# The second feed-forward level by seven products of halves in place of eight

## The chip, the cores and the metric

The kernel runs on one core of one Trainium2 chip. The metric is the device time of one execution in microseconds, the median over runs. Before the change three runs took 691.23 us (median), 689.8 us and 694.35 us.

## What is computed

An attention block of a recurrent kind (4 batches, 8 heads, 768 time steps, head size 40) is followed by a feed-forward block. Its output, seen as a matrix of 3072 tokens by 320, is the input x of the second block:

```python
for t in range(S):
    y[:, :, t] = einsum('bhd,bhde->bhe', rt, state)
    Sa = einsum('bhde,bhe->bhd', state, at)
    state = state * wt - einsum('bhd,bhe->bhde', Sa, bt) + einsum('bhd,bhe->bhde', vt, kt)
x = y.transpose(0, 2, 1, 3).reshape(B * S, H * D)      # 3072 x 320
h = x @ w_in                                           # 320 x 2048, given in float64
g = h * (1 / (1 + exp(-h)))
return g @ w_out                                       # 2048 x 320, given in float64
```

The last line is the second feed-forward level: per 256 tokens a product of 256 x 2048 by 2048 x 320, in fp32.

## The kernel before

The 768 time steps are cut into `NN` = 12 chunks of `C` = 64 steps. One chunk has 4 batches x 64 = 256 tokens. A chunk goes through these functions:

- `load` and `load_r` fetch the inputs of a chunk from HBM with SP's queue (from L402). k and b land in the staging tile `kbv` (L412).
- `prepare` (from L456) forms running products of w with two scans on VectorE (L473 and L491), multiplies a, k and b by them (L500 and L510; L510 reads `kbv` and writes the packed tile `kb`), and lets TensorE form products of `kb` with a (L528), mask them (L577), multiply them with v (L592) and transpose k and b (L617). Its result `R` goes to one of three buffers.
- `special` and `inverse` solve the triangular systems of a chunk: `special` for the first three chunks one at a time, `inverse` for two chunks at a time, with 19 steps of VectorE each (L643 and L644).
- `merge`, `chain` and `read` (from L940) put the inverse together, carry the state from chunk to chunk (L1046 to L1174) and read the output y (L1204 to L1269). L1269 writes y, and `bring` moves it by way of HBM to the tile `xt`, channels on partitions.
- `moe` (from L1332) is the feed-forward block. Its first level, in four groups of 512 hidden units, is L1340 and L1353 on TensorE and the Silu on ScalarE (L1363), which writes the tile `gts`: 16 blocks of 128 hidden units by 256 tokens. Its second level (`second`, L1380) takes, for each half `b` of 128 tokens, 16 products of a 128 x 128 block of `gts` (the stationary operand) with a 128 x 320 block of `wo` (the moving operand), summed in PSUM; each half is copied out to the tile `ot` (L261 on VectorE, in the last chunk L257 on ScalarE) and stored (L1399).
- `weights` turns w_in and w_out from float64 words into fp32 on the chip, in ten units, during the first chunks (from L314). `wo` is the converted w_out.

All these functions do not issue instructions; they add operations to a `Plan`, each with the engine, the keys of what it reads and writes, and the PSUM rooms that it needs. The order in which they are issued is written out by hand: `ORDER` (L74) lists the numbers of the operations, and `SLOTS` gives each room its buffer. Every engine and each DMA queue takes its own operations in this order and waits, at each, for what it needs. So a wait on one engine holds up all that is listed behind it on that engine.

fp32 products show in the profile as two TensorE instructions each, and each of these has its own load of the stationary operand (the rows named PEld).

Of the kernel before, what the change touches and what calls it, by code (L numbers as in the profile page):

```python
# [10 lines left out]
F32 = mybir.dt.float32  # L11
# [119 lines left out]
"""  # L131

SLOTS = """
02010313103013023201121220321321331102201331232212021000300010012010102103230113332111021202013323111302020230
10211001211003132011132330130003220300213021120013103110133031021231131031100212001201232130132032033001101332
32011022330030001301001320110132012332222001102003101210203231232113030320232121101130100132012
"""


@with_exitstack  # L140
def kernel(
    ctx: ExitStack,
    tc: tile.TileContext,
    aT: bass.AP,
    kT: bass.AP,
    bT: bass.AP,
    wT: bass.AP,
    rT: bass.AP,
# [14 lines left out]
    T = B * C  # L163
# [292 lines left out]
    def prepare(n):  # L456
# [1152 lines left out]
```

## Time and profile before

| what | number |
|---|---|
| median of three runs | 691.23 us (689.8 to 694.35) |
| span of the profiled execution | 690.3 us |
| instructions | 27487 |
| ScalarE busy | 198.4 us (29%) |
| mean granted TensorE clock | 0.994 |
| bytes read from and written to HBM | 60.03 and 14.35 MB |
| mean busy share of the 16 DMA engines, SP's queue | 36.0% |

How to read the lines of the profile that follow: a group is a line of the kernel, an engine, an operation, the tile written and the tiles read, the shape and the count; behind the bar stand the busy time of the group in us, the mean duration of one in ns, and how long the engine was idle just before, with what ended that. For TensorE `128*128` is the size of the stationary operand (rows by columns) and `128x320` that of the moving one. Times on TensorE are latencies of single instructions that run overlapped; the busy time of a group counts overlapped time once. PE is the matmuls, PEld the weight loads. In the timeline a row is the start in us, the time covered, and the group, with neighbours of one kind merged (`x48`).

### The profile page before, as it was taken

How to read it: one execution, taken by the hardware profiler on the slowest of the kernel's cores; microseconds unless marked ns; L12 is line 12 of the kernel's file. 1: busy time of each engine (PE TensorE's matmuls, PEld its weight loads, DVE VectorE, ACT ScalarE, POOL GpSimd, SP SyncE). 2: the span in 40 equal slices, each digit the busy share in tenths (PEclk: the TensorE clock that was granted, in tenths of full speed). 3: DMA queues.
4: the chain of work that ended last, by engine and by line, in shares of the span. 5: the costliest groups of instructions: out<-in, count | busy, mean ns of one | idle time of the engine just before them, and what ended most of it. 6: DMA issues, size and time to landing. Idle time of an engine off the chain costs nothing.

```text
span 690.3 us, 27487 instructions
## 1 busy us (share of the span) xinstructions
PE 656.6 (95%) x12794; PEld 531.4 (77%) x12794; DVE 420.9 (61%) x632; ACT 198.4 (29%) x254; POOL 13.0 (2%) x30
## 2 busy tenths in 40 slices
PE   1589999999999999999999999999999999999996
PEld 1467788788778778878778778778788778788774
DVE  7998988984894558954538962639854773011000
ACT  4562364343214332214222222222223122121020
POOL 3000110000000000000000000000000000000000
PEclk9999999999999999999999999999999999999999
DMA  9945385725255462561730672352542214111100
GB/s 291 296 125 138 92 257 168 183 37 133 78 140 120 103 167 63 128 159 27 194 103 14 193 166 66 104 134 74 152 86 65 74 35 105 28 45 34 42 2 22
DMA packets 113282, 76.64 MB, mean 111 GB/s; under 512 B 61154, under 2 KB 109589, under 8 KB 112520
## 3 DMA queue, kind: packets, MB, share of 16 engines
q1 hardware_dynamic: 110436, 63.71, 36.0%
q0 software_dynamic: 2224, 10.63, 4.7%
q8 instruction: 102, 1.67, 1.0%
q10 hardware_dynamic: 500, 0.46, 0.3%
q14 instruction: 20, 0.16, 0.1%
HBM read 60.03 MB, written 14.35 MB: 108 GB/s over the span
## 4 chain that ended last, share of the span: by engine, by line
PE 87%; DVE 7%; DMA 2%; issue 1%; SPq 1%; ACT 1%; POOL 1%; DVEq 0%; ACTq 0%; POOLq 0%
PE pair L1380 31%; PE pair L1340 24%; PE pair L1353 7%; PE pair L1204 4%; PE pair L528 3%; PE pair L1258 3%; PE pair L1158 2%; PE pair L617 2%; PE pair L1046 2%; PE pair L592 2%; PE pair L1243 2%; PE pair L1070 1%; PE pair L1101 1%; PE pair L890 1%; DVE kbv L473 1%
## 5 line engine op out<-in xcount | busy, mean ns | idle before, releaser
L1380 PE MATMUL pair<-wo,gts 128*128 128x320 f32 x768 | 215.8, 437 | 0.0
L1380 PEld LDWEIGHTS pair<-wo,gts 128*128 128x128 f32 x768 | 143.4, 190 | 58.0 <-issue 1.0
L1340 PE MATMUL pair<-xt,wi 128*128 128x256 f32 x768 | 175.8, 383 | 0.0
L1340 PEld LDWEIGHTS pair<-xt,wi 128*128 128x128 f32 x768 | 143.5, 190 | 22.1 <-issue 0.7
L1363 ACT ACTIVATE gts<-pair 128x1024 f32<-128x1024 f32 x48 | 47.6, 1026 | 91.2 <-PE pair L1353 84.1
L644 DVE TENSOR_REDUCE XI<-XI 128x64 f32<-128x512 f32 (+9 forms) x85 | 58.7, 690 | 2.9
L1216 DVE TENSOR_TENSOR lam<-pair,ml 128x1024 f32<-128x1024 f32 x22 | 26.4, 1220 | 46.6 <-PE pair L1204 29.4
L1353 PE MATMUL pair<-xt,wi 64*128 64x256 f32 x384 | 48.0, 389 | 0.8 <-DMA xt<-X 0.8
L261 DVE COPY ot<-pair 128x320 f32<-128x320 f32 x22 | 10.8, 489 | 57.0 <-PE pair L1380 49.4
L528 PE MATMUL pair<-a,kb 40*64 40x64 f32 x1536 | 30.1, 228 | 15.0 <-DVE a L500 13.4
L1353 PEld LDWEIGHTS pair<-xt,wi 64*128 64x128 f32 x384 | 35.3, 187 | 7.1 <-issue 2.0
L528 PEld LDWEIGHTS pair<-a,kb 40*64 40x64 f32 x1536 | 26.9, 141 | 17.2 <-issue 15.0
L643 DVE TENSOR_TENSOR XI<-XI,mi 128x1024 f32<-128x1024 f32 (+8 forms) x60 | 33.6, 560 | 5.1 <-DMA mi<-md 3.8
L510 DVE TENSOR_TENSOR kb<-kbv 128x512 f32<-128x512 f32 (+1 forms) x36 | 29.9, 862 | 6.6 <-PE pair L528 3.3
L630 ACT COPY kt<-pair 128x640 f32<-128x640 f32 x24 | 16.5, 695 | 56.1 <-PE pair L617 55.9
L1204 PEld LDWEIGHTS pair<-r,vut 40*64 40x64 f32 x1536 | 24.4, 135 | 5.2 <-issue 2.8
L473 DVE TENSOR_TENSOR_SCAN kbv<-wz,zt 128x1024 f32<-128x1024 f32 x12 | 27.5, 2292 | 0.6
L1204 PE MATMUL pair<-r,vut 40*64 40x64 f32 x1536 | 26.8, 220 | 1.0 <-DMA r<-in_rT 0.9
L491 DVE TENSOR_TENSOR_SCAN wz<-wz,zt 128x1024 f32<-128x1024 f32 x12 | 27.5, 2289 | 0.3
L259 ACT ACTIVATE vut<-pair 128x1024 f32<-128x1024 f32 (+1 forms) x13 | 12.5, 958 | 49.4 <-PE pair L1101 45.4
L643 DVE TENSOR_TENSOR XI<-XI,xs 128x1024 f32<-128x1024 f32 (+1 forms) x25 | 25.2, 1008 | 0.6
L937 ACT COPY mi<-XI 128x1024 f32<-128x1024 f32 x5 | 10.0, 2002 | 51.8 <-DVE XI L644 31.7
(160 smaller groups left out, 685.2 us busy)
## 6 DMA issues: line engine op xcount, KB each, us to landing
wz<-in_wT SPq DMA_DIRECT2D x12, 512.0 KB
a<-in_aT SPq DMA_DIRECT2D x12, 512.0 KB
kbv<-in_bT SPq DMA_DIRECT2D x12, 512.0 KB
kbv<-in_kT SPq DMA_DIRECT2D x12, 512.0 KB
vut<-in_vT SPq DMA_DIRECT2D x48, 96.0 KB
r<-in_rT SPq DMA_DIRECT2D x48, 96.0 KB
vu<-in_v SPq DMA_DIRECT2D x24, 160.0 KB
xh<-lam SPq DMA_DIRECT2D x22, 160.0 KB
```

The lines of the kernel that those rows point to most:

```text
L473: nc.vector.tensor_tensor_scan(back(V), back(W[:, 2 : 2 + Q * C]), zt, 1.0, ALU.mult, ALU.add)
L491: nc.vector.tensor_tensor_scan(Z, Z, zt, 0.0, ALU.mult, ALU.add)
L510: TTn[engine].tensor_tensor(out=at_(kb, place(is_b, first), (576 * step, 4 // step), (128, 4), (1, C)), in0=blocks((kf, bf)[is_b]), in1=bl ...
L528: nc.tensor.matmul(room.tile[half(b), j, g * C : g * C + C], lhsT=kb[rows(j), place(is_b, q) : place(is_b, q) + C], rhs=A[rows(j), q * C : ...
L643: nc.vector.tensor_tensor(out=at_(tmp, 0, *dims), in0=x, in1=y, op=ALU.mult)
L644: nc.vector.tensor_reduce(out=out_, in_=at_(tmp, 0, *dims), axis=AX.X, op=ALU.add)
L1204: nc.tensor.matmul(pl.tile[half(1 - b if role else b), b, c * C : c * C + C], lhsT=vut[rows(b), role, hu, :], rhs=rs[rows(b), hh, :], star ...
L1216: lambda pl=pl, la=la: nc.vector.tensor_tensor(out=la.tile.rearrange("p (q t) -> p q t", q=Q), in0=pl.tile.rearrange("p a b -> p (a b)").r ...
L1340: nc.tensor.matmul(rooms[g].tile[:, f // 2, (f % 2) * T : (f % 2) * T + T], lhsT=wi[:, k, (4 * g + f) * 128 : (4 * g + f) * 128 + 128], rh ...
L1353: nc.tensor.matmul(rooms[g].tile[:, h, (f % 2) * T : (f % 2) * T + T], lhsT=wi3[half(h), g * 256 + (f % 2) * 128 : g * 256 + (f % 2) * 128 ...
L1363: nc.scalar.activation(out=gts[:, 4 * g * T : 4 * g * T + 4 * T], in_=rooms[g].tile.rearrange("p a b -> p (a b)"), func=AF.Silu)
L1380: nc.tensor.matmul(po[b].tile[:, 0, 0:DM], lhsT=g4[:, f, 128 * b : 128 * b + 128], rhs=wo[:, f, :], start=f == 0, stop=f == NF - 1,)
```

## The change

From chunk 1 on, the second level is done by Strassen's algorithm (in Winograd's form). The 256 x 2048 matrix of gated values is cut into four blocks, by half of the hidden units and half of the tokens, and w_out into four of 1024 x 160. Instead of eight products of such blocks there are seven. Each is eight matmuls of a 128 x 128 stationary block with a 128 x 160 moving block (`prod`, `block_`). VectorE forms four sums of blocks of `gts`, in place (`mixed` on `gs`), and puts the seven products together in `ot`, which now holds a whole chunk. Three sums of blocks of w_out are made once, after chunk 0, into the tiles `tw` and `raw0` (`parts_`), and a fourth in place in `wo`. Chunk 0 keeps the old second level.

Room for the new tiles comes from two others. `kbv` goes: k and b are loaded straight into `kb`, with four transfers each, and VectorE multiplies there in place; of `kbv` there stays the tile `ws` for the scan. `Rs` has two buffers instead of three. The output of a chunk is stored by two transfers of 160 KB instead of four of 80 KB. The keys of `gts` are split by token half. `ORDER` and `SLOTS` are new, with 1568 operations in place of 1437.

```diff
-    kbv = sb.tile([128, 3, Q * C], F32, name="kbv")
+    ws = sb.tile([128, Q * C], F32, name="ws")
+    tw = sb.tile([128, 12 * HM], F32, name="tw")
...
-    Rs = ring("R", 3, Q * D)
+    Rs = ring("R", 2, Q * D)
...
-    ot = ring("ot", 1, DM)
+    ot = sb.tile([128, 2 * DM], F32, name="ot")
...
+            if dst is None:
+                for m in range(B):
+                    dma(
+                        lambda m=m, src=src, is_b=name == "b": nc.sync.dma_start(
+                            at_(kb, place(is_b, 4 * m), (2 * C, 4), (1, C)), src[m, n].rearrange("p (q c) -> p q c", q=4)
+                        ),
...
-                TTn[engine].tensor_tensor(
-                    out=at_(kb, place(is_b, first), (576 * step, 4 // step), (128, 4), (1, C)),
-                    in0=blocks((kf, bf)[is_b]),
-                    in1=blocks(V),
-                    op=ALU.mult,
-                )
+                x = at_(kb, place(is_b, first), (576 * step, 4 // step), (128, 4), (1, C))
+                y = at_(V, first * C, (4 * C * step, 4 // step), (C, 4), (1, C))
+                TTn[engine].tensor_tensor(out=x, in0=x, in1=y, op=ALU.mult)
...
+        def block_(half_, b, right, bank, i, first):
+            for f in range(8):
                 nc.tensor.matmul(
-                    po[b].tile[:, 0, 0:DM],
-                    lhsT=g4[:, f, 128 * b : 128 * b + 128],
-                    rhs=wo[:, f, :],
-                    start=f == 0,
-                    stop=f == NF - 1,
+                    po.tile[:, bank, col(i)],
+                    lhsT=g4[:, 8 * half_ + f, 128 * b : 128 * b + 128],
+                    rhs=right(f),
+                    start=first and f == 0,
+                    stop=f == 7,
+                    skip_group_check=True,
                 )
...
+        mixed(gs(0, 1), lambda: gs(0, 0), gs(0, 1), ALU.subtract, gk(0, 0), gk(0, 1))
+        prod(1, 1, made(2), [("T", 2)], 0, 2, True)
+        prod(0, 0, own(0, 0), lo, 0, 0)
+        prod(1, 0, own(1, 0), hi, 0, 1)
+        mixed(gs(1, 1), lambda: gs(1, 1), gs(0, 1), ALU.subtract, gk(0, 1), gk(1, 1))
+        mixed(gs(0, 0), lambda: gs(1, 1), gs(0, 0), ALU.add, gk(1, 1), gk(0, 0))
+        mixed(gs(1, 0), lambda: gs(1, 0), gs(1, 1), ALU.subtract, gk(1, 1), gk(1, 0))
+        last = ot[:, col(3)]
+        add("ACT", act(HM), lambda: nc.scalar.copy(out=last, in_=po.tile[:, 0, col(0)]), [(po, 0)], [("ot", 3)], 10 * n, [po])
+        mixed(ot[:, col(0)], lambda: po.tile[:, 0, col(1)], last, ALU.add, [(po, 0), ("ot", 3)], [("ot", 0)], HM, [po])
+        prod(0, 1, made(0), [("T", 0)], 1, 1, True)
+        prod(1, 1, made(1), [("T", 1)], 1, 2)
+        prod(0, 0, own(0, 1), lo, 1, 0)
+        prod(1, 0, own(1, 1), hi, 0, 0, True)
+        mixed(last, lambda: po.tile[:, 1, col(2)], last, ALU.add, [(po, 1)], [("ot", 3)], HM, [po])
+        mid = ot[:, HM : 3 * HM].rearrange("p (x d) -> p x d", x=2)
+        mixed(
+            mid, lambda: po.tile[:, 1, 0 : 2 * HM].rearrange("p (x d) -> p x d", x=2), last.unsqueeze(1).to_broadcast([128, 2, HM]), ALU.add,
+            [(po, 1), ("ot", 3)], [("ot", 1), ("ot", 2)], 2 * HM, [po],
+        )
+        mixed(last, lambda: po.tile[:, 1, col(0)], ot[:, col(2)], ALU.add, [(po, 1), ("ot", 2)], [("ot", 3)], HM, [po])
+        mixed(
+            mid, lambda: at_(po.tile[:, 0, :], 0, (2 * HM, 2), (1, HM)), mid, ALU.add, [(po, 0)], [("ot", 1), ("ot", 2)], 2 * HM, [po]
+        )
+        store()
...
+        mixed(part_(0, 0, 8), own(1, 1), own(0, 1), ALU.subtract, [*lo, *hi], [("T", 0)])
+        for f in (0, 4):
+            mixed(part_(1, f, 4), part_(0, f, 4), own(0, 0, f, 4), ALU.add, [*lo, ("T", 0)], [("T", 1)] + ["raw0"] * (f > 0), 4)
+            mixed(part_(2, f, 4), own(1, 0, f, 4), part_(1, f, 4), ALU.subtract, [*hi, ("T", 1)], [("T", 2), "raw0"], 4)
+        mixed(own(0, 1), own(0, 1), own(0, 0), ALU.subtract, [], lo)
```

`prod` numbers below follow the order of these lines: products 1 to 3 read the halves as the gate left them, products 4 to 7 read at least one sum.

More of the change, by code (lines that the diff above doesn't have):

```diff
@@ L300 @@
         "B": [("wo", c) for c in (1, 2)],
-        **{f"G{i}": [("gts", 2 * i), ("gts", 2 * i + 1)] for i in range(2)},
+        **{f"G{i}": [("gts", g, b) for g in (2 * i, 2 * i + 1) for b in range(2)] for i in range(2)},
     }
@@ L458, in prepare @@
         i3, i2 = n % 3, n % 2
-        (kf, bf, V), (kk, bk, vk) = [kbv[:, i] for i in range(3)], ("k", "b", "V")
+        V, vk = ws, "V"
+        kk, bk = ([(x, m) for m in range(B)] for x in "kb")
         W, A = wz[i3], at[i3]
@@ L536, in prepare @@
         pb_ = Room("pair", 2)
-        add("PE", 0.9, partial(between, 1, pb_), ["B", ("a", i3)], [pb_, ("sb", i2)], pri, [pb_], 128)
+        add("PE", 0.9, partial(between, 1, pb_), [*bk, ("a", i3)], [pb_, ("sb", i2)], pri, [pb_], 128)
         add("ACT", act(1024), lambda: copy("ACT", sbs[i2], by_two(pb_.tile), -1.0), [pb_], [("sb", i2)], pri, [pb_])
@@ L573, in prepare @@
         pk, sk = Room("pair", 2), Room("lam", 3)
-        add("PE", 0.9, partial(between, 0, pk), ["K", ("a", i3)], [pk], pri + 0.5, [pk, sk], 128)
+        add("PE", 0.9, partial(between, 0, pk), [*kk, ("a", i3)], [pk], pri + 0.5, [pk, sk], 128)
         def masked():
@@ L598, in sv @@
                 )
-        add("PE", 0.9, sv, [sk, ("v", i2, 0), ("v", i2, 1)], [pv, ("R", i3)], pri + 0.6, [pv, sk], 128)
+        add("PE", 0.9, sv, [sk, ("v", i2, 0), ("v", i2, 1)], [pv, ("R", i2)], pri + 0.6, [pv, sk], 128)
         add(
@@ L603, in prepare @@
             act(640),
-            lambda: nc.scalar.copy(out=Rs[i3][:, 0 : Q * D].rearrange("p (b c) -> p b c", b=2), in_=pv.tile[:, :, 0 : 8 * D]),
+            lambda: nc.scalar.copy(out=Rs[i2][:, 0 : Q * D].rearrange("p (b c) -> p b c", b=2), in_=pv.tile[:, :, 0 : 8 * D]),
             [pv],
-            [("R", i3)],
+            [("R", i2)],
             pri + 0.6,
@@ L624, in turn @@
                         )
-            add("PE", 0.5, turn, ["K", "B"], [pt, ("kt", i3, b)], pri + 0.7, [pt], 32, shape="T")
+            add("PE", 0.5, turn, [*kk, *bk], [pt, ("kt", i3, b)], pri + 0.7, [pt], 32, shape="T")
             add(
@@ L1060, in chain @@
             add("PE", 0.9, right, [("a", i3), "G"], [pa], pri, [pa], 128)
-            add("DVE", vec(640), total, [pa], [("R", i3)], pri, [pa])
+            add("DVE", vec(640), total, [pa], [("R", i2)], pri, [pa])
         pw_ = {part: Room("pair", 2) for part in halves(n)}
@@ L1076, in solve @@
                     )
-            add("PE", 0.9, solve, [*xkeys, ("R", i3)], [pu], pri, [pu], 128)
+            add("PE", 0.9, solve, [*xkeys, ("R", i2)], [pu], pri, [pu], 128)
             for b in range(2):
@@ L1122, in chain @@
             pw = pw_[part]
-            add("PE", 0.46 * l, partial(solve_t, part, pw), [*xp, ("R", i3)], [pw, *[("ut", m) for m in part]], p_, [pw], 64 * l)
+            add("PE", 0.46 * l, partial(solve_t, part, pw), [*xp, ("R", i2)], [pw, *[("ut", m) for m in part]], p_, [pw], 64 * l)
             add("ACT", act(512 * l), partial(turned, part, pw), [pw], [("ut", m) for m in part], p_, [pw])
@@ L1367, in moe, with gk @@
         xk = [[("xt", k + t, h) for h in range(H)] for k, t in ((0, 0), (1, 0), (2, 0), (2, 1))]
+        def gk(half_, b):
+            return [("gts", g, b) for g in (2 * half_, 2 * half_ + 1)]
         for g in (0, 2):
@@ L1371, in moe @@
             for i, x in enumerate((a_, b_)):
-                add("PE", 3.45, partial(full, g + i), [*xk[0], *xk[1], *w_(g + i)], [x, ("ff", n), ("gts", g + i)], pri + g + 0.1 * i, [x], 32, shape="F")
+                add("PE", 3.45, partial(full, g + i), [*xk[0], *xk[1], *w_(g + i)], [x], pri + g + 0.1 * i, [x], 32, shape="F")
             add("PE", 1.72, partial(rest, g), [*xk[2], *xk[3], ("wi3",)], [a_, b_], pri + g + 0.2, [a_, b_], 32, shape="R")
-            add("ACT", act(1024), partial(gate, g), [a_], [("gts", g)], 10 * n, [a_])
@@ L1375, in moe @@
-            add("ACT", act(1024), partial(gate, g + 1), [b_], [("gts", g + 1)], 10 * n, [b_])
-        po = [Room("pair", 5, 2) for _ in range(2)]
-        def second(b, part):
-            for f in range(4 * part, 4 * part + 4):
-                nc.tensor.matmul(
-                    po[b].tile[:, 0, 0:DM],
-                    lhsT=g4[:, f, 128 * b : 128 * b + 128],
-                    rhs=wo[:, f, :],
-                    start=f == 0,
-                    stop=f == NF - 1,
-                )
@@ L1388, in moe @@
-        for b in range(2):
-            for part in range(4):
-                need = sorted({("wo", c) for c in range(4 * part * DM // WS, ((4 * part + 4) * DM - 1) // WS + 1)})
-                add("PE", 2.14, partial(second, b, part), [("gts", part), ("ff", n), *need], [po[b]], pri + 4 + b + part * 0.1, [po[b]], 16, shape="F")
-            e = "ACT" if n == NN - 1 else "DVE"
-            add(e, vec(320), lambda b=b, e=e: copy(e, ot[0], po[b].tile[:, 0, 0:DM]), [po[b]], ["ot"], 10 * n, [po[b]])
+            add("ACT", act(1024), partial(gate, g), [a_], [("gts", g, b) for b in range(2)], 10 * n, [a_])
@@ L1394, in moe, with store, stored @@
+            add("ACT", act(1024), partial(gate, g + 1), [b_], [("gts", g + 1, b) for b in range(2)], 10 * n, [b_])
+        def store():
             e = "ACT" if n == NN - 1 else "SP"
             for m in range(2):
-                def stored(m=m, r0=(2 * m + b) * S + C * n, e=e):
-                    (nc.scalar if e == "ACT" else nc.sync).dma_start(out[r0 : r0 + C, :], ot[0][half(m)])
-                dma(stored, 80, ["ot"], [("out", n, b, m)], 10 * n + 9, e)
+                def stored(m=m):
+                    to = out.rearrange("(x s) d -> x s d", x=B)[2 * m : 2 * m + 2, C * n : C * n + C]
+                    (nc.scalar if e == "ACT" else nc.sync).dma_start(
+                        to.rearrange("b s d -> s b d"), ot[half(m)].rearrange("s (b d) -> s b d", b=2)
+                    )
+                dma(stored, 160, [("ot", i) for i in range(4)], [("out", n, m)], 10 * n + 9, e)
@@ new lines, in moe, with second @@
+        if n == 0:
+            po = [Room("pair", 5, 2) for _ in range(2)]
+            def second(b, part):
+                for f in range(4 * part, 4 * part + 4):
+                    nc.tensor.matmul(
+                        po[b].tile[:, 0, 0:DM],
+                        lhsT=g4[:, f, 128 * b : 128 * b + 128],
+                        rhs=wo[:, f, :],
+                        start=f == 0,
+                        stop=f == NF - 1,
+                    )
+            for b in range(2):
+                for part in range(4):
+                    need = sorted({("wo", c) for c in range(4 * part * DM // WS, ((4 * part + 4) * DM - 1) // WS + 1)})
+                    add("PE", 2.14, partial(second, b, part), [("gts", part, b), *need], [po[b]], pri + 4 + b + part * 0.1, [po[b]], 16, shape="F")
+                add("DVE", vec(DM), lambda b=b: nc.vector.tensor_copy(out=ot[:, DM * b : DM * b + DM], in_=po[b].tile[:, 0, 0:DM]), [po[b]], [("ot", 2 * b), ("ot", 2 * b + 1)], 10 * n, [po[b]])
+            store()
+            return
@@ new lines, in moe, with gs, col @@
+        po = Room("pair", 13, 2)
+        lo, hi = [("wo", c) for c in range(3)], [("wo", c) for c in range(2, 5)]
+        def gs(half_, b):
+            return g4[:, 8 * half_ : 8 * half_ + 8, 128 * b : 128 * b + 128]
+        def col(i):
+            return slice(HM * i, HM * i + HM)
+        def block_(half_, b, right, bank, i, first):
+            for f in range(8):
+                nc.tensor.matmul(
+                    po.tile[:, bank, col(i)],
[4 more added lines that the diff above has]
+                    skip_group_check=True,
+                )
@@ new lines, in own, with made, prod, mixed @@
+        def own(x, y):
+            return lambda f: wo[:, 8 * x + f, col(y)]
+        def made(t):
+            return lambda f: part_(t, f)
+        def prod(half_, b, right, keys, bank, i, first=False):
+            add("PE", 2.18, partial(block_, half_, b, right, bank, i, first), [*gk(half_, b), *keys], [(po, bank)], pri + 4 + bank, [po], 16, shape="F")
+        def mixed(to, x, y, op, r, w, cost=8 * 128, rooms=()):
+            add("DVE", vec(cost), lambda: nc.vector.tensor_tensor(out=to, in0=x(), in1=y, op=op), r, w, 10 * n, rooms)
@@ new lines, in moe, with part_, parts_, own @@
+        store()
+    def part_(t, f, n=1):
+        i = 8 * t + f
+        x, i = (tw, i) if i < 12 else (raws[0], i - 12)
+        x = x[:, HM * i : HM * i + HM * n]
+        return x.rearrange("p (f d) -> p f d", f=n) if n > 1 else x
+    def parts_():
+        lo, hi = [("wo", c) for c in range(3)], [("wo", c) for c in range(2, 5)]
+        def own(x, y, f=0, n=8):
+            return wo[:, 8 * x + f : 8 * x + f + n, HM * y : HM * y + HM]
+        def mixed(to, x, y, op, r, w, n=8):
+            add("DVE", vec(HM * n), lambda: nc.vector.tensor_tensor(out=to, in0=x, in1=y, op=op), r, w, 13)
+        mixed(part_(0, 0, 8), own(1, 1), own(0, 1), ALU.subtract, [*lo, *hi], [("T", 0)])
[3 more added lines that the diff above has]
+        mixed(own(0, 1), own(0, 1), own(0, 0), ALU.subtract, [], lo)
@@ L1477 @@
     with tc.If(flag > 0):
+        corner = wo[:, 0:8, HM : 2 * HM]
+        nc.vector.tensor_tensor(out=corner, in0=corner, in1=wo[:, 0:8, 0:HM], op=ALU.add)
         with tc.For_i(0, B * NN) as i:
```

29 lines of the change are left out of this document (18 added, 11 removed), and 118 rows, old and new, of the table ORDER.

## The prediction

> **What bounds the kernel now.** I read the page first, then busy time by stretches, then the groups of TensorE.
>
> ```profile
> PE 656.6 (95%) x12794; PEld 531.4 (77%) x12794; DVE 420.9 (61%) x632; ACT 198.4 (29%) x254; POOL 13.0 (2%) x30
> ...
> PE 87%; DVE 7%; DMA 2%; issue 1%; SPq 1%; ACT 1%; POOL 1%; DVEq 0%; ACTq 0%; POOLq 0%
> ```
>
> TensorE is busy for 95% of the span and carries 87% of the chain that ended last. The stretches (PE, PEld, DVE, ACT, POOL busy us, granted clock, DMA share) show where that holds.
>
> ```profile
> 34.50:51.80 17.30, 14.99 (x367) 11.73 (x363) 17.04 (x24) 10.60 (x15) 0.57 (x1) 0.90 0.44 125
> 86.30:103.50 17.20, 16.28 (x373) 14.05 (x372) 15.40 (x17) 11.91 (x13) 2.03 (x3) 1.00 0.82 256
> 207.00:310.00 103.00, 103.00 (x2257) 83.68 (x2250) 68.05 (x103) 29.62 (x41) 0.00 (x0) 1.00 0.49 123
> 310.00:414.00 104.00, 103.79 (x2058) 84.51 (x2056) 66.11 (x94) 30.17 (x42) 0.00 (x0) 1.00 0.46 116
> 620.00:690.30 70.30, 64.35 (x459) 49.12 (x458) 3.51 (x5) 6.86 (x9) 0.00 (x0) 0.99 0.09 24
> ```
>
> Until about 100 us VectorE is full (17.04 of 17.30) and TensorE has holes. After that TensorE has none (103.00 of 103.00, 103.79 of 104.00) at the full clock, with VectorE at about 65%. Two chunks take some 104 us there. So from 100 us on the time is the sum of what TensorE does, and a microsecond taken from it is a microsecond won as long as nothing makes it wait.
>
> ```profile
> L1380 PE MATMUL pair<-wo,gts 128*128 128x320 f32 x768 | 215.8, 437 | 0.0
> L1340 PE MATMUL pair<-xt,wi 128*128 128x256 f32 x768 | 175.8, 383 | 0.0
> L1380 PEld LDWEIGHTS pair<-wo,gts 128*128 128x128 f32 x768 | 143.4, 190 | 58.0 <-issue 1.0
> ```
>
> The second level (L1380) is the dearest group. Each of its 32 fp32 products per chunk shows as two instructions, each with its own weight load: 768 = 12 x 64.
>
> **The TensorE term.** The mean of 437 ns is a latency; what counts is the step from one instruction to the next. Differences between runs of unequal length give it (the timeline of TensorE: start, us, what).
>
> ```profile
> 334.27 13.19 PE L1380 MATMUL pair<-wo,gts 128*128 128x320 f32 x48
> ...
> 350.35 2.42 PE L1380 MATMUL pair<-wo,gts 128*128 128x320 f32 x8
> ...
> 358.23 3.72 PE L1340 MATMUL pair<-xt,wi 128*128 128x256 f32 x16
> ...
> 375.48 7.17 PE L1340 MATMUL pair<-xt,wi 128*128 128x256 f32 x32
> ```
>
> 320 columns: (13.19 - 2.42) / 40 = 269.3 ns. 256 columns: (7.17 - 3.72) / 16 = 215.6 ns. That is 0.838 ns a column and 1 ns besides, so 160 columns stream in 269.3 - 160 x 0.838 = 135.1 ns. The second level is 64 x 269.3 = 17.23 us a chunk now. After the change it is seven products of 8 matmuls, two instructions each: 112 x 135.1 = 15.13 us. The saving is 2.10 us a chunk, in 11 chunks **23.1 us**. Columns fall by an eighth, but weight loads rise from 64 to 112 a chunk, and no row of before has a 128-column load with so short a stream. That is the disputed cost. It is bounded by how long a load keeps its place.
>
> ```profile
> 334.27 0.30 PEld L1380 LDWEIGHTS pair<-wo,gts 128*128 128x128 f32 x2
> ...
> L1380 PEld LDWEIGHTS pair<-wo,gts x2: 186/188/189, 334.3 to 334.4; 128*128 128x128 f32 x2
> ```
>
> ```profile
> 323.87 1.31 PEld L1158 LDWEIGHTS pair<-vu,kt 128*40 128x40 f32 x64
> ...
> 347.39 1.16 PE L528 MATMUL pair<-a,kb 40*64 40x64 f32 x64
> ...
> 348.31 1.03 PEld L1046 LDWEIGHTS pair<-G,a 40*64 40x64 f32 x64
> ...
> L528 PE MATMUL pair<-a,kb 40*64 40x64 f32 x1536 | 30.1, 228 | 15.0 <-DVE a L500 13.4 <-ACT wi L337 1.1 <-issue 0.3
> L1046 PEld LDWEIGHTS pair<-G,a 40*64 40x64 f32 x704 | 11.5, 135 | 2.2 <-issue 2.0 <-ACT X L257 0.2
> L1158 PEld LDWEIGHTS pair<-vu,kt 128*40 128x40 f32 x704 | 14.7, 122 | 1.0 <-issue 0.8
> ```
>
> The first fence is the timeline at the start of a run and the durations of the two loads in it, the second the timeline and the groups of short loads. Two loads of 0.19 us cover 0.30 us together, so the second began 0.30 - 0.19 = 0.11 us after the first: a 128-column load holds its place about 110 ns, and the rest of its 190 ns is latency. The short loads say the same. L1158 uses two parts of the array in turn: (1.31 - 0.122) / 63 x 2 = 38 ns for 40 columns, though each load is shown as 122 ns. L1046 uses four: (1.03 - 0.135) / 63 x 4 = 57 ns for 64. That is 0.8 ns a column, about 108 ns at 128. So the bounds of the step are 135 ns (load hidden under the stream, 25 ns to spare) and 190 ns (the recorded length counts). I take 135. The nearest row where load and stream are about equal is L528, 64 columns by 64: (1.16 - 0.228) / 63 x 4 = 59 ns against a stream of 55, 4 ns over; 139 ns here would cost 4.9 us of the saving, inside the range.
>
> [...]
>
> **The rest of TensorE.** The written order has 36 runs of second-level operations before and 36 after, so entries into a run (the exposed 0.11 us) cost the same. Chunk 0 stays as it is: 0.
>
> **VectorE.** It gets, per chunk, four sums of 1024 elements, three of 160 out of PSUM and two of 320, for two copies of 320.
>
> ```profile
> L643 DVE TENSOR_TENSOR XI<-XI,mi 128x1024 f32<-128x1024 f32 x15 | 18.3, 1220 | 0.2
> L1056 DVE TENSOR_TENSOR R<-pair,R 128x640 f32<-128x640 f32 x11 | 9.0, 821 | 6.1 <-PE pair L1046 6.0
> L261 DVE COPY ot<-pair 128x320 f32<-128x320 f32 x22 | 10.8, 489 | 57.0 <-PE pair L1380 49.4 <-DMA out<-ot 4.0 <-DMA r<-in_rT 1.9
> L473 DVE TENSOR_TENSOR_SCAN kbv<-wz,zt 128x1024 f32<-128x1024 f32 x12 | 27.5, 2292 | 0.6
> L667 DVE COPY xs<-XI 128x256 f32<-128x256 f32 x5 | 1.9, 376 | 0.0
> L667 DVE COPY xs<-XI 128x128 f32<-128x128 f32 x5 | 1.3, 270 | 0.1
> ```
>
> 4 x 1.22 + 3 x 0.30 (between the last two rows) + 2 x 0.49 - 2 x 0.49 = 5.8 us a chunk, 64 us in all. The sums of the weights, once, are two of 1280 (about 1.5 us) and four of 640 (0.82): 6.3 us. VectorE goes to 491 us, 73% of a span of 669; in the stretch 310 to 414, 66 + 12 = 78 of some 100 us. It fits, but it is a queue, and there is a new loop: products 1 to 3 read the gated halves, sums 2 to 4 overwrite those in place, products 5 to 7 read the sums. What covers it is the products between. In chunk 10, whose order is tightest (1, 2, 4, 5, 6), product 5 comes two products (32 x 0.135 = 4.3 us) after product 1, against 1.22 us of sum. A sum is late only when a scan (2.29 us) or a step of the block inverse (two instructions of up to 1.22) stands ahead of it, and behind that sum stand the evictions and masks that TensorE's next steps need. Bounds: 0 and one uncovered sum per chunk, 13 us; I take 2 us, because over 20 us in 100 stay free.
>
> **Loads.** k and b land in kb itself, in four transfers each for one, and VectorE multiplies in place at the price of L510.
>
> ```profile
> L412 SPq DMA_DIRECT2D kbv<-in_bT x12: 389/506/1020, 2.0 to 470.3; - x12
> ...
> SPq L412 <- DVE kb L510: 25.3, 4, 9.2
> ```
>
> Six more issues of 0.5 us make 3 us of SP's queue per chunk of 52, less two stores of the output. The transfers now wait until TensorE has read the last chunk's kb (L528, L617), where they waited for VectorE's product. Behind them on SP stand the stores and the hops of xh that feed the first level. The cover is that loads are ordered a chunk or more ahead. I take 0; without that cover, two of the longest waits (9.2 us) reach TensorE, 18 us. R's ring falls from three to two buffers: same cover, 0.
>
> **Start and end.** Ahead of the second L1269 of chunk 0 (which releases its first level) the new order has dropped one scan step, one mask and six weight conversions and taken up five other operations.
>
> ```profile
> L339 DVE TENSOR_SCALAR wo<-wo 128x1024 int32<-128x1024 int32 x4 | 2.8, 690 | 0.1
> ```
>
> That is 2.6 (a scan and what goes with it) + 5 x 1.22 + 2 x 0.69 = 10.1 us out and 0.82 + 2 x 1.22 + 2 x 0.69 = 4.6 us in: 5.4 us less on the full engine, but the dropped work comes soon after and the transfers of the weights are re-ordered too. Bounds -6 and +6; I take -1.
>
> ```profile
> 666.85 17.49 PE L1380 MATMUL pair<-wo,gts 128*128 128x320 f32 x64
> 684.38 0.43 ACT L257 COPY ot<-pair 128x320 f32<-128x320 f32 x1 [3.88 <-PE pair L1380]
> 684.84 1.12 ACTq L1399 DMA_DIRECT2D out<-ot  x2
> ```
>
> At the end one sum of 320 (0.49) stands where ACT's copy (0.43) stood, and two transfers carry 160 KB instead of 80: +0.3.
>
> **Sum.** 690.3 - 23.1 + 2 + 0.3 - 1 = 668.5 us of span; the median of the three runs is 0.9 over the profiled span, so **669 us**, own range 662 to 677.
>
> **Rivals.**
> Waits eat half of the saving (0.14). One sum a chunk is uncovered, 11 x 1.22 = 13.4 us in place of my 2: 681 us, 676 to 690. For it: the loop through VectorE and its in-order queue. Against it: the free quarter of VectorE and the products in between.
> The load sets the pace (0.12); this is the slower side. The place is the 112 loads a chunk; it decides from 17.23 us / 112 = 153.8 ns a step upward. At 190 ns: 21.3 us a chunk, 4.05 x 11 = 45 us more, 736 us. For it: 190 ns stands on every load. Against it: 0.30 us for two loads, and 38 and 57 ns above. [...]
> The start is won as well (0.08): all 6 us of VectorE's early work and no waits: below 662, about 660. For it: VectorE's 17.04 of 17.30; against it: the holes there also wait for weights.
>
> **How the numbers follow.** Forecast 0.66, the rivals 0.14, 0.12, 0.08. 660 to 686 takes in the forecast, the start and two thirds of the waits. A measurement of this kernel can tell about 1% from no change, here 684.3 and 698.1. Faster: 0.66 + 0.08 + 0.08 of the waits = 0.82, less 0.02 for unknown loads: 0.80. Slower 0.10 (most of the pace rival); the same 0.10.
>
> **What would show it.** Right: some 1232 instructions of 128x160 with a step near 135 ns (a run of 16 in about 2.4 us), TensorE's busy time near 634 us, VectorE's near 490, no wait of TensorE on a sum over 1 us. Wrong: a step over 154 ns, or waits of TensorE on VectorE or on kb's loads that add up to over 10 us after 100 us.

## The result, and the profile after

In one comparison the kernel before took 690.51 us (median of 4 runs, 689.46 to 694.35) and the changed one 711.94 us (4 runs, 708.33 to 713.65). The ratio is 1.029, with a 95% interval of [1.024, 1.033]: slower, where 669 us was forecast. The profiled execution of the changed kernel took 713.54 us, with a span of 711.7 us. Ratios further down are of fast runs alone (e10's aside, which had only one), against the kernel before in the same comparison, while medians are of all runs: of e1's five runs the profiled one (687.79 us) and one more were slow and the fast ones took 677.32 to 684.17 us, and e9's profiled run was slow too.

Lines of the page of the changed kernel: the busy times, the granted clock in 40 slices, the chain.

```profile
PE 651.4 (92%) x13322; PEld 579.6 (81%) x13322; DVE 485.4 (68%) x717; ACT 199.6 (28%) x263; POOL 12.5 (2%) x30
...
PEclk9999899999899999999989999998999999999998
...
PE 70%; DVE 11%; DMA 7%; SPq 5%; issue 3%; ACT 2%; POOL 0%; DVEq 0%; ACTq 0%; POOLq 0%
```

VectorE is busy for as long as forecast (485 of 490 us). TensorE is not at 634 us but at 651, and carries 70% of the chain in place of 87%. The clock has slices of 8 in the middle, which it had not before.

The stretches of before again. Columns: the stretch, its length, busy time and count of PE, PEld, DVE, ACT and POOL, the granted clock, DMA share, GB/s.

```profile
207.00:310.00 103.00, 98.55 (x2084) 88.05 (x2082) 79.23 (x110) 29.12 (x39) 0.00 (x0) 1.00 0.46 115
310.00:414.00 104.00, 97.23 (x2289) 88.52 (x2288) 70.48 (x103) 25.63 (x38) 0.00 (x0) 0.97 0.41 104
414.00:520.00 106.00, 100.92 (x2037) 92.41 (x2038) 66.78 (x99) 26.33 (x38) 0.00 (x0) 0.95 0.41 99
```

The last of these stretches in the kernel before:

```profile
414.00:520.00 106.00, 106.00 (x2324) 86.76 (x2322) 62.30 (x90) 28.04 (x37) 0.00 (x0) 1.00 0.41 102
```

TensorE was busy throughout in the middle of the kernel before. Now 4 to 7 us of each hundred are idle, and in two of the three stretches the granted clock is 0.95 to 0.97: TensorE stops, and part of its work runs at a lower clock (0.50 in 180.2 to 187.0, 364.5 to 371.3, 415.7 to 419.1 and 477.2 to 484.0 us).

The new groups (L1439 is the products, L1458 every sum on VectorE), and the waits of TensorE from 100 us on (what waits, for what: us in all, number, longest):

```profile
L1458 DVE TENSOR_TENSOR gts<-gts 128x1024 f32<-128x1024 f32 x44 | 53.6, 1219 | 32.4 <-ACT gts L1377 15.9
L1458 DVE TENSOR_TENSOR ot<-pair,ot 128x160 f32<-128x160 f32 (+1 forms) x55 | 21.4, 388 | 72.4 <-PE pair L1439 46.3
```

```profile
PE pair L1439 <- DVE ot L1458: 11.3, 8, 2.9
PE pair L1439 <- ACT ws L535: 4.2, 1, 4.2
PE pair L1218 <- ACT R L618: 2.6, 1, 2.6
```

TensorE does not wait for the sums of the gated halves (`gts`), but for the sums that take its own results out (`ot`), and VectorE in turn has stood 46.3 us waiting for products. One such place, chunk 4 in the timeline:

```profile
359.91 2.44 PE L1439 MATMUL pair<-wo,gts 128*128 128x160 f32 x16
362.39 0.29 ACT L1468 COPY ot<-pair 128x160 f32<-128x160 f32 x1 [17.68 <-PE pair L1439]
362.71 0.33 DVE L1458 TENSOR_TENSOR ot<-pair,ot 128x160 f32<-128x160 f32 x1 [6.13 <-ACT ot L1468]
362.95 1.21 DVE L1458 TENSOR_TENSOR gts<-gts 128x1024 f32<-128x1024 f32 x1
364.08 1.22 DVE L529 TENSOR_TENSOR kb<-kb,ws 128x1024 f32<-128x1024 f32 x1
365.33 0.70 DVE L268 COPY ZQ<-pair 32x512 f32<-32x512 f32 x1
366.06 0.32 DVE L1458 TENSOR_TENSOR ot<-pair,ot 128x160 f32<-128x160 f32 x1
366.54 3.81 PE L1439 MATMUL pair<-wo,gts 128*128 128x160 f32 x13 [4.18 <-ACT ws L535]
```

Here is `ORDER` in chunk 4: 742, 750, 743, 744, 751, 752, 753 are products 1, 4, 2, 3, 5, 6, 7; 748 is the copy at L1468; 749 and 754 to 757 are the sums that put the output together; the other numbers between are other work.

```
742 750 743 744 ... 745 1022 751 ... 746 ... 945 752 748 1027 940 749 747 1023 941 754 753 ... 755 756 757
```

Read from the top: the run of 16 is product 6, which writes bank 1 of the pair of PSUM banks `po`. The copy needs only product 2 in bank 0, whose matmuls ended long before, and yet it waits 17.68 us, until product 6 has ended. The first sum waits 6.13 us for the copy; behind it in VectorE's queue stand a sum of gated halves, k times its running product, another copy and the next output sum (754). Product 7 (bank 0) starts 0.16 us after that sum has ended, although 754 reads bank 1. (The profile puts this wait down to ScalarE's L535, which ended at the same moment; but it writes `ws`, which no product reads, and a wait for several things is put down by inference.) Product 7 also reads the sum of gated halves in this list, which ended at 364.16 us, so the last 2.4 us of its wait are for 754. So it looks as if whatever touches the tile `po` waits for what other engines did with it before, in the written order, also in the other bank. In the kernel before each half of a chunk had a pair of its own and used one bank of it.

The time, worked out from the starts of consecutive matmuls between the first of chunk 1's first level and the last one: an interval over 0.48 us is a stop, counted less 0.2 us; "half clock" is what intervals in windows of half clock take above the same intervals elsewhere; all in us.

| kernel | second level | other TensorE work | stops (number) | half clock | sum |
|---|---|---|---|---|---|
| before | 196.3 | 352.8 | 0.3 (1) | 0 | 549.4 |
| after | 172.7 | 357.2 | 26.6 (21) | 10.6 | 567.1 |

The second level gained 23.6 us, the stops cost 26.3, the half clock 10.6, the other work 4.4, the start 0.7 (chunk 1 begins at 135.2 us, before at 134.5) and the end 3.0: 21.4 us more of span.

### The profile page after: what moved, and what is told of

Same layout as the page of the kernel before. It is cut to its first block, busy times and chain, and to the rows that moved or that the text cites. A ratio compares the mean times of both kernels' runs of the same rounds, so it can differ in the third digit from the quotient of the medians.

```text
span 711.7 us, 28708 instructions
## 1 busy us (share of the span) xinstructions
PE 651.4 (92%) x13322; PEld 579.6 (81%) x13322; DVE 485.4 (68%) x717; ACT 199.6 (28%) x263; POOL 12.5 (2%) x30
## 3 DMA queue, kind: packets, MB, share of 16 engines
q8 instruction: 106, 1.74, 1.0%
## 4 chain that ended last, share of the span: by engine, by line
PE 70%; DVE 11%; DMA 7%; SPq 5%; issue 3%; ACT 2%; POOL 0%; DVEq 0%; ACTq 0%; POOLq 0%
PE pair L1439 21%; PE pair L1354 19%; PE pair L1367 5%; PE pair L1218 3%; PE pair L1272 3%; PE pair L542 3%; PE pair L1412 3%; DVE XI L657 2%; DMA gts<-in_w_in 2%; DMA kb<-in_bT 2%; DMA kb<-in_kT 2%; SPq L421 2%; PE pair L631 1%; DVE XI L658 1%; DVE kb L529 1%
## 5 line engine op out<-in xcount | busy, mean ns | idle before, releaser
L1439 PE MATMUL pair<-wo,gts 128*128 128x160 f32 x704 | 108.6, 313 | 10.3 <-DVE ot L1458 6.1
L1439 PEld LDWEIGHTS pair<-wo,gts 128*128 128x128 f32 x704 | 103.2, 200 | 11.9 <-issue 7.4
L1458 DVE TENSOR_TENSOR gts<-gts 128x1024 f32<-128x1024 f32 x44 | 53.6, 1219 | 32.4 <-ACT gts L1377 15.9
L1458 DVE TENSOR_TENSOR ot<-pair,ot 128x160 f32<-128x160 f32 (+1 forms) x55 | 21.4, 388 | 72.4 <-PE pair L1439 46.3
L1377 ACT ACTIVATE gts<-pair 128x1024 f32<-128x1024 f32 x48 | 46.8, 1024 | 70.9 <-PE pair L1367 70.8
L1439 PE MATMUL pair<-tw,gts 128*128 128x160 f32 x264 | 40.9, 309 | 6.3 <-DVE ot L1458 5.1
L1439 PEld LDWEIGHTS pair<-tw,gts 128*128 128x128 f32 x264 | 37.5, 194 | 8.1 <-DVE ot L1458 6.3
L1439 PE MATMUL pair<-raw,gts 128*128 128x160 f32 x264 | 40.7, 304 | 0.0
L529 DVE TENSOR_TENSOR kb<-kb,ws 128x512 f32<-128x512 f32 (+1 forms) x36 | 29.9, 864 | 14.9 <-DMA kb<-in_kT 9.5
L1439 PEld LDWEIGHTS pair<-raw,gts 128*128 128x128 f32 x264 | 37.3, 192 | 0.9 <-issue 0.3
L1468 ACT COPY ot<-pair 128x160 f32<-128x160 f32 x11 | 3.2, 294 | 92.7 <-PE pair L1439 78.7
```

Source lines behind the costliest of these rows:

```text
L529: TTn[engine].tensor_tensor(out=x, in0=x, in1=y, op=ALU.mult)
L1377: nc.scalar.activation(out=gts[:, 4 * g * T : 4 * g * T + 4 * T], in_=rooms[g].tile.rearrange("p a b -> p (a b)"), func=AF.Silu)
L1439: nc.tensor.matmul(po.tile[:, bank, col(i)], lhsT=g4[:, 8 * half_ + f, 128 * b : 128 * b + 128], rhs=right(f), start=first and f == 0, sto ...
L1458: add("DVE", vec(cost), lambda: nc.vector.tensor_tensor(out=to, in0=x(), in1=y, op=op), r, w, 10 * n, rooms)
```

## The experiments

The theory after the result (T1): `po` is one thing to the framework that puts the waits into the program, so products and the reading of products take turns across banks in the written order, which was planned as if the banks were apart. Rivals: the loop of sums in place (T2), the loads straight into `kb` (T3), and slowness of the new order as such (T4).

**e1: products nobody reads.** The copy and the five output sums read `wi` in SBUF instead of `po`.

```diff
-lambda: nc.scalar.copy(out=last, in_=po.tile[:, 0, col(0)])
+lambda: nc.scalar.copy(out=last, in_=wi[:, 0, col(0)])
...
-        mixed(ot[:, col(0)], lambda: po.tile[:, 0, col(1)], last, ALU.add, [(po, 0), ("ot", 3)], [("ot", 0)], HM, [po])
+        mixed(ot[:, col(0)], lambda: wi[:, 0, col(1)], last, ALU.add, [(po, 0), ("ot", 3)], [("ot", 0)], HM, [po])
```

> The changed kernel, but the ScalarE copy and the five output sums of each chunk read their product operand from a part of w_in in SBUF instead of the PSUM tile, so that no product waits for an evacuation and no evacuation for a product; the output is not the reference's. All engines' work stays. Theory 1 (the lost time is the wait of products for evacuations and of evacuations for products that share one two-bank PSUM tile): of the some 29 us of TensorE stops after 100 us at most 10 are left, the half clock behind them goes too, 680 us (672 to 690). Theory 2 (the loop products - sums of the gate halves - products sets the pace): 700 to 712, the stops stay. Theory 3 (k and b loaded straight into the operand tile come late, and VectorE's queue waits behind them): 702 to 712.

684.17 us, ratio 0.980 [0.978, 0.983]. Its waits of TensorE, and the stretch that stood at 97.23 above:

```profile
PE pair L1218 <- ACT R L618: 2.5, 1, 2.5
PE pair L1115 <- ACT X L264: 1.8, 1, 1.8
PE pair L1412 <- DVE wo L359: 1.1, 1, 1.1
```

```profile
310.00:414.00 104.00, 103.05 (x2328) 94.32 (x2327) 75.75 (x114) 29.24 (x41) 0.00 (x0) 0.97 0.44 113
```

No wait of L1439 is left; stops fall from 26.6 to 7.6 us. All work of the change is in this kernel, in the same order, except that these six instructions do not read PSUM: that reading makes 19.0 us of the stops, and T4 does not explain them. The half clock was expected to go with the stops and did not: 10.0 us in the profiled run, where the changed kernel has 10.6 (and e4 below 8.4). The experiment does not yet say what share of the stops would stand if the banks were apart; the copy in chunk 4 above, e5 and e7 bear on that.

**e2: products 4 to 7 without the sums.** They take their stationary blocks from `wi`; the sums of halves are still made.

```diff
-                    lhsT=g4[:, 8 * half_ + f, 128 * b : 128 * b + 128],
+                    lhsT=wi[:, bank, 128 * f : 128 * f + 128] if summed else g4[:, 8 * half_ + f, 128 * b : 128 * b + 128],
```

> The changed kernel, but products 4 to 7 of each chunk take their left operand from w_in instead of the summed halves of gts, so that no product waits for a sum of halves; the sums are still made, the output is not the reference's. Theory 1 (shared PSUM tile): 700 to 712, the stops before products behind an evacuation stay. Theory 2 (the sums of halves set the pace): 680 us (672 to 690). Theory 3 (k and b late): 702 to 712.

709.77 us, ratio 1.024 [1.019, 1.028]; stops 25.6 us, where the changed kernel has 26.6.

```profile
PE pair L1439 <- DVE ot L1458: 15.5, 9, 4.2
```

The stops stay where they were, so T2 is not the cause.

**e3: k and b through a staging tile again**, as before the change (one of the new weight tiles gives up its room, so product 4 and half of product 5 read unsummed blocks).

```diff
-                            at_(kb, place(is_b, 4 * m), (2 * C, 4), (1, C)), src[m, n].rearrange("p (q c) -> p q c", q=4)
+                            kq[:, int(is_b), 4 * C * m : 4 * C * m + 4 * C].rearrange("p (q c) -> p q c", q=4), src[m, n].rearrange("p (q c) -> p q c", q=4)
```

> The changed kernel, but k and b land in a staging tile of 8 KB and VectorE multiplies them from there into the operand tile, as before the change, with the order unchanged; to make room, product 4 and half of product 5 use plain quarters of w_out, and two sums of weights are left out at the start (under 3 us of VectorE), so the output is not the reference's. Theories 1 and 2: 705 to 713, the stops of TensorE stay where they were. Theory 3 (k and b late): below 698, VectorE's waits for DMA after 100 us (some 15 us in the changed kernel) go to under 5 us and TensorE's stops fall with them.

710.47 us, ratio 1.024 [1.015, 1.032]. The row that answers to L1439's, and VectorE's wait for k, which in the changed kernel is the second row:

```profile
PE pair L1442 <- DVE ot L1461: 12.7, 8, 4.2
...
DVE kb L532 <- DMA kq<-in_kT: 3.8, 1, 3.8
```

```profile
DVE kb L529 <- DMA kb<-in_kT: 9.5, 3, 5.9
```

VectorE waits 5.7 us less for k, and TensorE's stops are 24.7 us, 1.9 less than they were. T3 is not the cause; the waits of VectorE were covered.

**e4: e1 and e2 together.**

> The edits of the two kernels before this one together: evacuations read SBUF, products 4 to 7 read w_in, so the second level has no wait on VectorE or ScalarE at all except for product 1 to 3 on the gates; the output is not the reference's. Theories 1 and 2 both: 674 us (667 to 682), which is the prediction's sum of 668.5 and a few stops from elsewhere. Theory 3, or a TensorE that is slower by itself in the 160-column products: 695 or more.

684.34 us, ratio 0.986 [0.981, 0.991]: e1's time, so the sums add nothing even where nothing else stops TensorE. The expectation missed by 10 us: stops of 7.8 and half clock of 8.4 us are left with no wait on the second level at all.

**e5: a new order for the second level alone.** 157 of the 1568 numbers of `ORDER` are moved, those of the second level of chunks 1 to 11, so that the copy and the sums stand between products that TensorE has in hand and ahead of long work on VectorE; the computation is whole. Chunk 4 then reads:

```diff
-742 750 743 744 ... 745 1022 751 ... 746 ... 945 752 748 1027 940 749 747 1023 941 754 753 ... 755 756 757
+750 740 742 743 744 748 ... 745 1007 751 ... 747 749 753 746 752 945 ... 754 ... 755 894 756 757
```

> The changed kernel computed in full, with a new written order in which only products, sums, copies and evacuations of the second level of chunks 1 to 11 have moved (157 of 1568 operations); in it no evacuation of a chunk is written between two of its products unless the next product really needs the space or other TensorE work stands in between, and the sums of halves come before the evacuations on VectorE. Theory 1 (products and evacuations wait for each other because both banks are one tile to the recorder, and the order did not know it): TensorE's stops after 100 us fall from 29 to some 10 us and the half clock behind them to under 4 us; 680 us (673 to 687), near the 677 to 689 of the kernel whose evacuations read SBUF, and faster than before the change. Theory 2 (the true waits of evacuations for products, or of products for sums, cost the time, and these are all still there): 700 or more.

695.53 us (12 runs), ratio to before 1.003 [1.000, 1.006]: 16 of the lost 21 us come back from the order alone, so reading these banks is not dear in itself; its place in the order is. Stops are 14.3 us in place of 26.6. The expected 680 was missed. What is left stands in its timeline and its waits:

```profile
175.80 0.80 DVE L269 TENSOR_SCALAR vu<-pair 64x640 f32<-64x640 f32 x1
176.64 0.70 ACT L265 ACTIVATE vu<-pair 64x640 f32<-64x640 f32 x1 [4.92 <-DVE vu L269]
177.35 0.69 ACT L617 COPY R<-pair 128x640 f32<-128x640 f32 x1
178.09 0.33 PE L1217 MATMUL pair<-r,vut 40*64 40x64 f32 x4 [3.15 <-ACT R L617]
```

```profile
PE pair L1217 <- ACT R L617: 3.2, 1, 3.2
PE pair L1059 <- issue: 2.5, 1, 2.5
PE pair L988 <- issue: 1.4, 1, 1.4
```

ScalarE waits 4.92 us for VectorE to have read the same pair, though both only read, and each another half of the partitions (both banks of them; e9's expectation below, which speaks of the other bank, has this wrong). Both also write `vu`; that a shared tile in SBUF makes them wait isn't likely, since in the changed kernel ScalarE (L1377) and VectorE (L1458) five times wrote parts of `gts` at the same time. The taking of turns seems to hold for two readers of a pair too, and TensorE stands behind it. The "issue" waits are of another kind, told at the end.

**e6, e9, e10, e11: other orders of the whole work.** 635 numbers are moved in e6 and 619 in e11, so that stops of every part of the kernel are looked at, in e11 also such that windows with little work on the array become rare. The edit is `ORDER` (and `SLOTS`) alone. All four missed the times expected of them (675, 682, 684 and 684 us).

> As the kernel before this one, but every operation on TensorE, VectorE and ScalarE from some 130 us on may have moved in the written order. Theory 1: the last stops of the other stages go too (the 2.9 us before the two look products of chunk 2 among them), 675 us (668 to 683), at most 8 us under the kernel with only the second level moved. Theory 2: 698 or more.

> The changed kernel computed in full, in one more written order of all of TensorE's, VectorE's and ScalarE's work from some 130 us on. It keeps three things apart: products and evacuations of one PSUM tile; reads of one PSUM tile by ScalarE and VectorE (in the second-level order ScalarE's copy of u at 171.7 us waited 4.9 us for VectorE's read of the other bank, and TensorE 3.2 us behind it); and long runs of short matmuls (in the kernel with everything moved TensorE stopped inside such runs nine times for 0.6 to 2.0 us, 11 us together, with nothing awaited, each time 192 rows past a multiple of 256 recorded instructions). If these three are what is left of the lost time: stops after 100 us under 7 us, 682 us (676 to 688), faster than before the change by some 1%. If the 160-column products cost more than their steps show, or VectorE's load sets the pace: 692 to 700, as in the last two orders.

> As the kernel before this one, with another order made by the same three rules from another start. If the rules are what counts and not the one order: within 4 us of the kernel before this one, 684 us (677 to 690). If the gain hangs on one lucky order: 690 to 700.

> The changed kernel computed in full, in an order that keeps, beside the three rules of the two kernels before, a fourth: no stretch of 3.4 us of short matmuls alone. In all runs so far 31 of 34 half-clock windows after 100 us stood behind a window of 3.41 us in which TensorE's streamed columns, weighed by the share of its rows and columns in use, came to under 1450 (a run of sixteen products of 160 columns counts 2560, a run of 64 matmuls of 40 rows and 64 columns 640), stops or not. If this and the stops inside short runs are what held the last orders at 694: at most one half-clock window after 100 us, stops under 8 us, 684 us (678 to 690), faster than before. If the half clock goes by something else, or the 160-column steps cost more than they show: 692 to 700.

| kernel | median us (runs) | ratio to before | second level | other | stops (number) | half clock | sum |
|---|---|---|---|---|---|---|---|
| e1 | 684.17 (5) | 0.980 [0.978, 0.983] | 171.9 | 355.7 | 7.6 (9) | 10.0 | 545.3 |
| e4 | 684.34 (4) | 0.986 [0.981, 0.991] | 171.9 | 357.5 | 7.8 (10) | 8.4 | 545.5 |
| e5 | 695.53 (12) | 1.003 [1.000, 1.006] | 172.4 | 358.8 | 14.3 (15) | 8.7 | 554.2 |
| e6 | 696.56 (7) | 1.008 [1.004, 1.012] | 172.6 | 362.5 | 13.8 (17) | 3.4 | 552.3 |
| e9 | 695.82 (12) | 1.003 [1.000, 1.006] | 174.2 | 362.2 | 7.0 (8) | 8.1 | 551.5 |
| e10 | 709.25 (4) | 1.026 [1.021, 1.030] | 174.1 | 363.3 | 13.7 (16) | 3.1 | 554.3 |
| e11 | 692.53 (12) | 1.000 [0.997, 1.002] | 175.1 | 363.3 | 9.0 (10) | 0.0 | 547.4 |

The last five columns are of the one profiled execution each. e9 had one run of 1282.66 us, which nothing here explains, and of e10 only the profiled run (695.44 us) is accounted for; its others took 706.82, 711.68 and 760.51 us, at mean granted clocks of 0.970, 0.974 and 0.846 (the profiled one at 0.990), and its ratio of 1.026 rests on them (the profiled run alone is 1.006 of the kernel before), so what that order costs is not settled. e11 is the best whole kernel, the same as before within the interval:

```profile
310.00:414.00 104.00, 101.97 (x2247) 91.86 (x2235) 77.48 (x113) 28.51 (x40) 0.00 (x0) 1.00 0.43 111
414.00:520.00 106.00, 104.54 (x2135) 93.73 (x2136) 75.71 (x107) 28.42 (x39) 0.00 (x0) 1.00 0.45 112
```

No half clock is left in the middle, and few stops. Of the 21.2 us of the second level (196.3 - 175.1), 8.7 go to stops and 10.5 to the other work of TensorE. Half of these 10.5 lies at the changes from one group of matmuls to the next and half inside runs of one group, counted by the same starts. The order changes group 259 times from chunk 1 on, where the kernel before does so 243 times, which is too few more to account for it; the cause was not taken apart. No version here beats the kernel before with the whole computation.

**e7 and e8: the stop by itself.** The kernel before, whole, with copies put into its second half of a chunk in chunks 2 to 10: ScalarE reads 64 columns of the other bank of the pair into which TensorE is summing, 5 times in e7 and 14 times in e8.

```diff
+                if 2 <= n <= 10 and (b, f) == (1, 10):
+                    for _ in range(5):
+                        nc.scalar.copy(out=held_, in_=po[1].tile[:, 1, 0:64])
```

> The kernel of before the change, with nine stops of TensorE put in: in chunks 2 to 10, ten f into the second half's sum, five ScalarE copies of 64 unused columns of the PSUM tile's other bank. A copy of 160 columns took 294 ns and one of 640 took 695, so one of 64 is put at 0.21 us, five at 1.1 us. If the two banks of a tile are held apart: no stop, 691 us as before. Theory 1 (one tile, products wait for readers of the other bank): nine stops of some 1.3 us, 702 us (699 to 706), with no half clock at them. If any stop brings the half clock: 9 times 1.7 to 3.4 us more, 717 to 733.

> As the kernel before this one, with fourteen copies at each place in place of five, 3.0 us by the same rows. Banks held apart: 691 us. Theory 1: nine stops of some 3.2 us, 29 us of stops; if the clock does not depend on them 720 us (716 to 724); if a stop of this length is followed by 3.4 to 6.8 us at half clock, as in the changed kernel, each costs 1.7 to 3.4 us more: 735 to 751.

e7: 705.58 us, ratio 1.020 [1.017, 1.023]. e8: 742.33 us, ratio 1.074 [1.071, 1.077]. One of the nine places, in e7 and then in e8, and in e8 the windows of this stop and behind it, and of another of the nine, in chunk 7, and behind it:

```profile
247.94 1.19 ACT L1383 COPY held__117<-pair 128x64 f32<-128x64 f32 x5 [4.88 <-PE pair L1384]
249.18 1.34 PE L1384 MATMUL pair<-wo,gts 128*128 128x320 f32 x4 [1.27 <-ACT held__117 L1383]
```

```profile
245.46 3.38 ACT L1383 COPY held__117<-pair 128x64 f32<-128x64 f32 x14 [4.88 <-PE pair L1384]
248.89 2.41 PE L1384 MATMUL pair<-wo,gts 128*128 128x320 f32 x4 [3.46 <-ACT held__117 L1383]
```

```profile
245.40:249.00 3.60, 0.14 (x2) 0.11 (x2) 1.00 (x2) 2.97 (x14) 0.00 (x0) 1.00 0.50 125
249.00:252.40 3.40, 3.40 (x48) 2.15 (x52) 0.00 (x0) 0.00 (x0) 0.00 (x0) 0.50 0.01 2
...
526.80:530.40 3.60, 0.21 (x1) 0.00 (x0) 1.44 (x2) 2.94 (x14) 0.00 (x0) 1.00 0.25 65
530.40:533.80 3.40, 3.32 (x12) 2.20 (x12) 0.00 (x0) 0.02 (x1) 0.00 (x0) 1.00 0.00 0
```

The copies touch nothing that TensorE writes (it sums in bank 0), and still ScalarE waits for the matmuls and the matmuls for ScalarE: this is T1's taking of turns in a kernel that has nothing of the change. The profile puts both waits down to semaphores (4.88 us of ScalarE; 1.27 us of TensorE in e7 and 3.46 us in e8). No run here shows two engines on two banks of one tile at once, so what the chip would do with it isn't shown. And a stop can have two prices. In e7 nine stops of 1.7 us, from start to start, cost 14 us in all (9 x 1.4 is 13) and no half clock follows (the mean granted clock is 0.985, in the runs of the kernel before 0.981 to 1.000). In e8 nine of 3.9 us cost 51 us, of which the stops themselves are 33 (9 x 3.9, less the 0.27 of a step each). The rest, 18 us, is the clock: eight of the nine stops are followed by 3.4 us (four times) or 6.8 us (four times) at a granted clock of 0.50, 41.0 us in all, whose half, 20.5 us, is the upper bound of what is lost there. The ninth, at 526.8 us, is as long and is followed by none.

## Why the prediction was wrong

- **The step of 135 ns: right.** The row shows a run by itself:

```profile
304.41 2.34 PE L1439 MATMUL pair<-wo,gts 128*128 128x160 f32 x16
```

  2.34 us for 16 is the forecast run of 2.4, and the second level gained 23.6 us against 23.1. The rival in which the load sets the pace did not come about: its 190 ns a step would make 3.0 us of these 16, though the loads at L1439 are still recorded with means of 192 to 200 ns.
- **The rest of TensorE, 0: too low.** 4.4 us after, 10.5 in e11. That the number of runs in the order is the same (36 before and after by the traces; e11 has 49) said too little.
- **VectorE, 491 us: right** (485.4). The free quarter was there and did not help, since it lies where VectorE waits for products.
- **Waits through VectorE, bounds 0 to 13, took 2: this is the step that failed**, in size and in its mechanism. I looked for what is late in the loop of the sums, and e2 shows that loop to cost at most 1.0 us of stops. Left out was the other way through the same queue: that the results are taken out of PSUM while the same tile is being written. The prediction costed the three sums out of PSUM by their time alone, 0.30 us each, and not as steps that TensorE and VectorE must take in turn. Before, a pair held the one sum of a half and was read once, when it was whole; in the change one pair serves all seven products of a chunk, and is read amid their making. The stops are 26.6 us where 2 were forecast, above the upper bound, and 19.0 of them go when the results are not read from PSUM (e1). Then there are 10.6 us of half clock, for which the sum had no term: it was priced throughout at the clock of before, which was that of an order without stops. Three of the four half-clock stretches stand behind stops of the products of 2.8 to 4.5 us; since e1 and e4 have 10.0 and 8.4 us of half clock without these stops, at other places, they are not its only cause.
- **Loads straight into kb, 0: right** (e3). **R's ring, 0**: not tried by itself.
- **Start, -1, bounds -6 to +6:** +0.7 by the start of chunk 1's first level. **End, +0.3: too low, +3.0.** Four sums stand at the end, one behind the other, where one was counted; that adds 0.9 us between the last matmul and the transfers. The other 2.1 lie behind: the span ends 7.6 us after the transfers of 160 KB start, where it ended 5.5 us after those of 80 KB.

```profile
698.79 3.56 PE L1439 MATMUL pair<-wo,gts 128*128 128x160 f32 x25
702.38 1.73 DVE L1458 TENSOR_TENSOR ot<-pair,ot 128x160 f32<-128x160 f32 x4 [7.92 <-PE pair L1439]
704.15 1.43 ACTq L1401 DMA_DIRECT2D out<-ot  x2
```

- **The signs.** "No wait of TensorE on a sum over 1 us" failed at once (2.9 us at L1458), and "over 10 us of waits on VectorE" was met. The rival with half the saving eaten had the place nearly right (VectorE's queue) and the mechanism wrong, and no rival made waits dear enough to turn the sign.

## What to carry to other kernels

Where several results share one tile of PSUM, list who writes and who reads it in the written order, over all its banks, and read the order as strictly serial: a reader between two products can be a wait of TensorE (11.3 us in eight waits of the changed kernel; 1.7 us a stop in e7, where the reads were of the other bank) unless TensorE has other work in the order there. (A tile of its own for each bank was not run.) Saved matmul time counts only in an order that keeps TensorE fed, and a stop of some 4 us can cost twice: itself and the half clock (0.50 for 3.4 or 6.8 us) that stood behind eight of nine in e8. Before costing a change at its arithmetic, remove the reading of its results as in e1: this gives what the saving is worth if the order could be made free (here 2%), and the rest is a question of order, which none of the five other orders tried here solved.

## What the runs showed of the hardware that was not expected

**The clock.** Half clock also came where TensorE had only two short stops, of 0.5 and 0.4 us as the table counts them. In e1:

```profile
320.00:324.00 4.00, 3.17 (x145) 2.88 (x140) 3.39 (x4) 2.32 (x4) 0.00 (x0) 1.00 0.03 7
324.00:328.00 4.00, 3.88 (x121) 3.57 (x113) 3.36 (x4) 3.56 (x7) 0.00 (x0) 0.51 0.01 4
```

TensorE is busy for 3.17 of 4.00 us, with short matmuls that use a part of the array's rows and columns, and the clock behind is 0.51. In e8 and in the changed kernel the recorded changes of the clock lie whole multiples of 3.41 us apart, and the half-clock stretches of both are 3.4 or 6.8 us long. With the streamed columns of a window of 3.41 us weighted by the share of rows and columns of the array that they use, 33 of 34 half-clock stretches of the twelve kernels up to e10 (e11's expectation counted 31) lie behind a window of under 1450 (360, 1280, 715 and 709 in the changed kernel), but only 24 of nearly 2000 other windows; in e11 four windows of some 1210 to 1400 passed without, so the bound is not sharp. The ninth stop of e8 fits: on the grid of these changes that stop fell across two windows, which kept 1600 and 2240 such columns, where the windows ahead of the eight others had at most 1280. That these columns decide is an estimate from the counts; only e11's order, made by it, bears on it, with 0.0 us of half clock.

**Pauses inside a run.** In e6, TensorE pauses for 1.19 us inside a run of 64 equal short matmuls and waits for nothing that the profile shows:

```profile
171.17 0.74 PE L1114 MATMUL pair<-X,R 64*40 64x64 f32 x35
173.10 0.65 PE L1114 MATMUL pair<-X,R 64*40 64x64 f32 x29 [1.19 <-issue]
```

In every run that has such pauses inside a group (all but e8) they fall within one of 192 past a multiple of 256 recorded TensorE instructions (in e6, among others, at 6592, 7104, 9152, 9663, 12736, 19648 and 21952; in the changed kernel at 5568, 6080 and 9408). The page of the changed kernel has this row for a queue of instructions (packets, MB, share):

```profile
q8 instruction: 106, 1.74, 1.0%
```

1.74 MB in 106 packets is 16 KB each, and about 251 of its 26644 instructions (102 packets for 25588 before). That the queue brings them is taken from these counts. TensorE goes on 2.2 to 3.1 us after such a packet's start (2.2, 2.5 and 2.8 us at the three places of the changed kernel). My estimate from these numbers is that there a long stretch of short matmuls ran ahead of its own code; it is read from the counts and wasn't tried by an experiment.
